# Four layers of linear and sliding-window attention with gradients, rewritten as streams of token tiles with transposes by DMA

## The chip, the cores and the metric

The kernel runs on one core of one Trainium2 chip. Times are device microseconds (us) of one execution. The kernel before takes 4126.97 us (median of 3 runs, 4115.88 to 4130.27). "PE" is the matrix engine, "PEld" its weight loads, "DVE" the vector engine, "ACT" the scalar engine, "POOL" the third elementwise engine, "SP" an engine that only issues DMAs. DMA shares are of the core's 16 DMA engines. SBUF and PSUM are the two memories in which the kernel's tiles live: DMAs load into SBUF, and PE's results go to PSUM. A "slab" is what one head group needs of q, k, v or a gradient for all tokens; the "ring" holds the transposed q, k and v of the last tiles.

## The reference

Four residual layers, A, B, A, B, on x of 2048 tokens by 640 features (32 heads of 20), with the same weights in both A layers and in both B layers. The kernel computes the output and the gradients of x and of the four weight matrices for a given output gradient, in bf16.

```python
def _A_ref(x, wqkv, wo):                    # linear attention
    q, k, v = split(x @ wqkv)               # (cut: reshape to heads)
    phi = lambda t: jnp.where(t > 0, t + 1, jnp.exp(t)) + 1e-6
    pq, pk = phi(q), phi(k)
    kv = jnp.einsum("bhsd,bhse->bhde", pk, v)
    z = jnp.einsum("bhsd->bhd", pk)
    o = jnp.einsum("bhqd,bhde->bhqe", pq, kv) / (jnp.einsum("bhqd,bhd->bhq", pq, z)[..., None] + 1e-6)
    return merge(o) @ wo

def _B_ref(x, wqkv, wo):                    # causal attention, window of 256 tokens
    scores = jnp.einsum("bhqd,bhkd->bhqk", q, k) * (Dh ** -0.5)
    mask = (idx[:, None] - idx[None, :] >= 0) & (idx[:, None] - idx[None, :] < 256)
    p = softmax(where(mask, scores, -1e9))
    return merge(jnp.einsum("bhqk,bhkd->bhqd", p, v)) @ wo

x = x + _A_ref(_layernorm(x), A_wqkv, A_wo)
x = x + _B_ref(_layernorm(x), B_wqkv, B_wo)
x = x + _A_ref(_layernorm(x), A_wqkv, A_wo)
x = x + _B_ref(_layernorm(x), B_wqkv, B_wo)
# outputs: x and, by jax.vjp with grad_out, the gradients of A_x, A_wqkv, A_wo, B_wqkv, B_wo
```

A token tile is 128 tokens, so there are 16 of them. In sliding attention a "unit" is one token tile for a group of four heads: 8 x 16 = 128 units a layer, each looking at up to three key tiles.

## The kernel before

It is a row of stages. Each stage runs over all 16 tiles and leaves its result in memory for the next one.

```python
def run(self):
    self.prep_weights()                 # pads and transposes all weights, stores them for later
    self.A_forward(0); self.B_forward(1); self.A_forward(2); self.B_forward(3)
    ...
    self.B_backward(3, first=True);  self.A_backward(2, first=True)
    self.B_backward(1, first=False); self.A_backward(0, first=False)
```

Nearly every transpose is a PE instruction into PSUM and a copy out of it. This is the one ahead of the backward projection:

```python
for f0 in range(0, QTT, fch):           # 15 blocks of 128x128 per tile, 8 per PSUM tile
    psT = pspool.tile([P, fch, P], BF, name="dqT_ps")
    self.transposes(psT, [dqkv[:, tt, f * P:(f + 1) * P] for f in range(f0, f1)])   # PE
    ...                                 # copy to SBUF by DVE or ACT
```

The exception is attention backward. There the score gradients `ds` are transposed by DMA from SP's queue, 12 blocks of 128x128 a unit, and the product that needs them comes three units after the scores:

```python
def dscore(u, half, ps):
    ...
    if half == 1:
        dsT_of[u] = pe.tile([P, 12, P], BF, name="dsT", bufs=4)
        nc.sync.dma_start_transpose(out=dsT_of[u][:, 0:4 * nkt, :], in_=ds_of[u][:, 0:4 * nkt * P])
...
load(0)                                 # seven slabs of 512 KB, from POOL's queue
for s in range(n + 3):
    if s < n and units[s][1] == 4 and units[s][0] + 1 < G:
        load(units[s][0] + 1)           # the next head group's slabs
    ...
    if 0 <= s - 3 < n:
        dq(s - 3, ps_o.tile([P, 3, 4, HPAD], F32, name="acc"))    # needs dsT of unit s-3
```

The weight gradients of each layer are computed when that layer's backward runs. The first layer of a pair writes its part to memory, the second reads it and adds.

The softmax here doesn't subtract the row's maximum and nothing guards it: scores larger than these inputs give would overflow.

## Time and profile before

The profiled execution took 4152.7 us. The table gathers the stages that the argument uses. "Busy" is the time in which an engine executed, "clock" the mean granted clock of PE as a fraction of full speed.

| stage | us | what it shows |
|---|---|---|
| whole | 4152.7 | PE 69%, DVE 51%, ACT 33%, clock 0.707 |
| sliding attention, forward, two times | 340, 360 | PE 65% and 62%, clock 0.50, DMA 0.12 and 0.15 |
| sliding attention, backward, two times | 499, 500 | PE 67%, clock 0.50, DMA 0.91 |
| one of the weight gradients | 73 | PE 91%, clock 0.94 |

The first lines of the profile's page, kernel before: busy time by engine, and the span in 40 equal slices, in tenths.

```profile
PE 2862.4 (69%) x28268; PEld 1667.8 (40%) x28268; DVE 2122.0 (51%) x5628; ACT 1367.2 (33%) x2440; POOL 428.7 (10%) x651
PEclk6978855569687555865555898689955555997799
DMA  8345611043455110489998323311599897223221
```

No engine is full over the whole. The slices with clock digit 5 are the four attention stages. Two of them coincide with a DMA row of 7 to 9 (backward), two with a row of 0 and 1 (forward). So the mean says little, and each stage is to be read by itself.

The view by window of the kernel before. Its columns are the window, its length, the busy time of PE, PEld, DVE, ACT and POOL with instruction counts, the clock, the DMA share and the bytes per time.

```profile
502.00:842.00 340.00, 220.54 (x2872) 129.63 (x2873) 187.71 (x1212) 169.10 (x128) 0.00 (x0) 0.50 0.12 37
1806.00:2305.00 499.00, 332.47 (x5344) 182.09 (x5344) 230.29 (x256) 259.38 (x641) 191.28 (x296) 0.50 0.91 158
2305.00:2378.00 73.00, 66.66 (x320) 31.67 (x321) 10.10 (x17) 0.00 (x0) 0.00 (x0) 0.94 0.16 54
```

In the backward window the only number near 1 is the DMA share. The DMA view of that same window says whose it is: the queues with their packets, megabytes and share of the 16 engines, and then the issues, with the median time to landing.

```profile
q1 hardware_dynamic: 188974, 47.92, 64.5%
q0 software_dynamic: 8064, 29.36, 25.8%
...
VT<-qkvT_131 POOLq DMA_DIRECT2D x8, 512.0 KB, 8.7
...
dsT<-ds SPq DMA_TRANSPOSE x128, 4.2
```

The first queue (SP's) carries the transposes (and one load of 2.6 MB) and the other the slab loads. Together they take 90.3% of 499 us, which is 450 us. The list of waits of PE in the window names the effect:

```profile
PE acc L875 <- DMA dsT<-ds: 114.7, 53, 9.3
PE sp L832 <- ACT e L847: 26.9, 49, 0.9
```

The columns are total us, times and the longest. PE waited 114.7 us of this stage for transposes.

### The profile page before, as it was taken

Reading aid. Unit: us, or ns where it says so; the run is one execution under the profiler, and the core shown is the slowest. Engines: PE = TensorE matmul, PEld = TensorE weight load, DVE = VectorE, ACT = ScalarE, POOL = GpSimd, SP = SyncE. Lnnn points to the kernel's source line nnn. Section 1 sums busy time; section 2 is a strip of 40 time slices with the busy share of each in tenths; the row PEclk is TensorE's granted clock in tenths of the full one; section 3 lists DMA queues with packets and bytes.
Section 4 is the critical chain, followed back from the end, with each engine's and each line's share of the span. In section 5 each row is a group of like instructions: output and inputs, shape, how many; then the busy total and the mean of one; then the engine's idle time right before and its main releaser. Section 6 shows DMA issues by size and latency. Waiting matters only on the chain. (4 is left out here: it accounts for less than half of the span.)

```text
span 4152.7 us, 70886 instructions
## 1 busy us (share of the span) xinstructions
PE 2862.4 (69%) x28268; PEld 1667.8 (40%) x28268; DVE 2122.0 (51%) x5628; ACT 1367.2 (33%) x2440; POOL 428.7 (10%) x651
## 2 busy tenths in 40 slices
PE   2767766667577666766677886578847677884577
PEld 2334433343343333433334464336423334453335
DVE  4765355556643555364445265435634444365526
ACT  1413345533033455144555120102245555120202
POOL 2000000000000000023333000000033342000000
PEclk6978855569687555865555898689955555997799
DMA  8345611043455110489998323311599897223221
GB/s 303 129 139 167 207 32 47 17 155 121 163 160 165 41 37 16 152 195 163 150 149 142 88 76 116 127 64 61 151 172 155 158 174 129 93 83 141 94 92 56
DMA packets 763051, 506.38 MB, mean 122 GB/s; under 512 B 574560, under 2 KB 728672, under 8 KB 760800
## 3 DMA queue, kind: packets, MB, share of 16 engines
q1 hardware_dynamic: 560304, 266.70, 28.4%
q10 hardware_dynamic: 186288, 176.42, 13.0%
q0 software_dynamic: 16128, 58.73, 6.1%
q8 instruction: 222, 3.64, 0.4%
q14 instruction: 109, 0.89, 0.1%
HBM read 232.72 MB, written 174.65 MB: 98 GB/s over the span
## 5 line engine op out<-in xcount | busy, mean ns | idle before, releaser
L866 DVE TENSOR_TENSOR ds<-sp,e 128x768 bf16<-128x768 f32 (+2 forms) x512 | 460.9, 907 | 516.7 <-PE sp L832 409.4
L847 ACT ACTIVATE e<-sp 128x768 bf16<-128x768 f32 (+2 forms) x512 | 392.1, 771 | 122.9 <-PE sp L832 100.6
L437 PE MATMUL sT_ps<-QTg,KTg 32*128 32x128 bf16 x2880 | 254.4, 296 | 162.0 <-DVE o_t L452 116.8
L832 PE MATMUL sp<-KT,QT 32*128 32x384 bf16 (+2 forms) x1024 | 284.7, 476 | 57.7 <-ACT e L847 32.6
L875 PE MATMUL acc<-ksl,dsT 128*128 128x20 bf16 x2880 | 124.8, 181 | 227.3 <-DMA dsT<-ds 226.9
L832 PE MATMUL sp<-VT,dOT 32*128 32x384 bf16 (+2 forms) x1024 | 246.4, 472 | 32.3 <-ACT e L847 21.1
L875 PEld LDWEIGHTS <-dsT 128*128 128x128 bf16 x2880 | 99.0, 105 | 349.5 <-DMA dsT<-ds 312.0
L551 PEld LDWEIGHTS <-dqT 128*128 128x128 bf16 x1920 | 186.3, 99 | 132.1 <-DVE dqT L545 29.9
L400 PE MATMUL qkvp_ps<-WBpad,hnT 128*128 128x512 bf16 x960 | 225.1, 386 | 1.6 <-ACT hnT L243 1.6
L851 POOL TENSOR_SCALAR_AFFINE_SELECT e<-e 128x512 bf16<-128x512 bf16 x256 | 162.1, 633 | 570.0 <-issue 525.4
L519 PEld LDWEIGHTS <-hn_bw 128*128 128x128 bf16 x1280 | 126.6, 99 | 197.4 <-issue 71.1
L547 ACT COPY dqT<-dqT_ps 128x896 bf16<-128x896 bf16 x64 | 58.0, 906 | 391.9 <-PE dqT_ps L159 304.3
L437 PEld LDWEIGHTS <-KTg 32*128 32x128 bf16 x2880 | 101.5, 112 | 198.8 <-DVE o_t L452 141.9
L291 PE MATMUL qkv_ps<-WA,hnT 128*128 128x512 bf16 (+1 forms) x640 | 149.6, 374 | 45.0 <-ACT vv L299 17.5
L551 PE MATMUL dh_ps<-WqTB,dqT 128*128 128x320 bf16 x960 | 139.6, 305 | 25.5 <-DMA WqTB<-WqTB 14.7
L551 PE MATMUL dh_ps<-WqTA,dqT 128*128 128x320 bf16 x960 | 140.4, 305 | 22.9 <-DVE dqT L545 10.3
L904 ACT ACTIVATE dqkv<-acc 128x80 bf16<-128x80 f32 x256 | 60.8, 238 | 257.9 <-PE acc L875 256.6
L855 POOL TENSOR_SCALAR_AFFINE_SELECT e<-e 128x512 bf16<-128x512 bf16 x224 | 141.8, 633 | 0.0
L875 PEld LDWEIGHTS <-e 128*128 128x128 bf16 x2880 | 103.6, 106 | 94.7 <-issue 79.5
L451 DVE RECIPROCAL linv<-sT_ps 128x4 f32<-128x4 f32 x256 | 46.8, 183 | 176.1 <-PE sT_ps L448 174.7
L875 PE MATMUL acc<-qsl,ds 128*128 128x20 bf16 x2880 | 134.0, 179 | 0.9 <-DVE ds L866 0.5
L875 PE MATMUL acc<-dosl,e 128*128 128x20 bf16 x2880 | 130.9, 181 | 4.7 <-ACT dqkv L904 4.6
(2500 smaller groups left out, 5699.9 us busy)
## 6 DMA issues: line engine op xcount, KB each, us to landing
qkvp_126<-qkvp_slab SPq DMA_DIRECT2D x16, 768.0 KB, 3.6
qkvp_130<-qkvp_slab ACTq DMA_DIRECT2D x16, 768.0 KB, 3.4
qkvT_127<-qkvT_slab ACTq DMA_DIRECT2D x32, 256.0 KB, 5.2
qkvT_131<-qkvT_slab SPq DMA_DIRECT2D x32, 256.0 KB, 4.3
dN<-tmp_dN SPq DMA_DIRECT2D x2, 2560.0 KB, 15.3
tmp_dNT<-dNT SPq DMA_DIRECT2D x2, 2560.0 KB, 7.9
dNT<-tmp_dNT ACTq DMA_DIRECT2D x2, 2560.0 KB, 13.3
WqTA<-WqTA SPq DMA_DIRECT2D x2, 2400.0 KB, 8.9
```

Source lines behind the costliest of these rows:

```text
L291: nc.tensor.matmul(ps[:, 0:w_], lhsT=hnT[:, k, tt * P:(tt + 1) * P], rhs=WA[:, k, c0:c1], start=(k == 0), stop=(k == DT - 1))
L400: nc.tensor.matmul(ps, lhsT=hnT[:, k, tt * P:(tt + 1) * P], rhs=WB[:, k, c0:c0 + 512], start=(k == 0), stop=(k == DT - 1))
L437: nc.tensor.matmul(sT[:, hh, i * P:(i + 1) * P], lhsT=KTg[HPAD * hh:HPAD * (hh + 1), kt * P:(kt + 1) * P], rhs=QTg[HPAD * hh:HPAD * (hh + ...
L519: nc.tensor.matmul(pss[m][:, 0:c1 - c0], lhsT=hn[:, tt, m * P:(m + 1) * P], rhs=dqkv[:, tt, c0:c1], start=(tt == 0), stop=(tt == TT - 1))
L551: nc.tensor.matmul(ps[:, ci, 0:cw], lhsT=dqT[:, k, :], rhs=WqT[:, k, ci * cw:(ci + 1) * cw], start=(k == 0), stop=(k == QTT - 1))
L832: nc.tensor.matmul(ps[:, j, 0:nkt * P], lhsT=slabs[g][ta][r0:r0 + HPAD, b * P:(b + 1) * P], rhs=slabs[g][tb][r0:r0 + HPAD, k0 * P:(k0 + nk ...
L847: nc.scalar.activation(ev[:, 2 * half:2 * half + 2], ps[:, :, 0:nkt * P].rearrange("p h (i k) -> p h i k", k=P), ACT.Exp, scale=c_att)
L851: nc.gpsimd.affine_select(out=ev[:, :, nkt - 1, :], in_=ev[:, :, nkt - 1, :], compare_op=ALU.is_ge, fill=0.0, base=0, pattern=[[0, 4], [-1 ...
L855: nc.gpsimd.affine_select(out=ev[:, :, 0, :], in_=ev[:, :, 0, :], compare_op=ALU.is_ge, fill=0.0, base=-1, pattern=[[0, 4], [1, P]], chann ...
L866: nc.vector.tensor_tensor(out=dv[:, hs], in0=ps[:, :, 0:nkt * P].rearrange("p h (i k) -> p h i k", k=P), in1=ev[:, hs], op=ALU.mult)
L875: nc.tensor.matmul(acc[:, slot, hh, 0:DH], lhsT=lhsT, rhs=slabs[g][rhs_name][:, t, HPAD * hh:HPAD * hh + DH], start=(i == 0), stop=(i == l ...
L904: nc.scalar.mul(dqkv[:, b, 4 * g * DH:(4 * g + 4) * DH].rearrange("p (h d) -> p h d", d=DH), acc[:, 2, :, 0:DH], c_att)
```

## The change

The intent is to let neighbouring layers share the engines. While the sliding attention of one tile runs, the projections, the norm and the next layer's qkv of other tiles fill its gaps. PE's transposes and their PSUM copies go to DMA, the weights need no preparation, and the gradients of a weight's two layers are summed in PSUM at the end. The diff is nearly a new program. Here is its core.

```diff
@@ run @@
-        self.prep_weights()
-        self.A_forward(0)
-        self.B_forward(1)
-        self.A_forward(2)
-        self.B_forward(3)
...
+            self.seg_first(acc)                       # first half of layer 0
+            for l in (0, 2):
...
+                    self.seg_pair(l, mbd, acc)        # second half of A, all of B, first half of the next A
+        self.seg_do_first(3)                          # output gradient through wo
+        for l in (3, 1):
...
+                self.seg_attention_bwd(l, dqkv)
...
+                self.seg_B_to_A(l, dqkv, acc, dNT)
+            self.seg_A_to_B(l - 1, acc, dNT)
...
+        self.weight_grads((3, 1), self.out_dWB, self.out_dWoB)
+        self.weight_grads((2, 0), self.out_dWA, self.out_dWoA)
```

The forward pair. One step handles attention of tile b, and the other work (`plan`, in this order, with its distance in tiles) is fed in two pieces per head group:

```diff
+            plan = ((qkv, 2), (first_half, -2), (proj2, -1), (proj1, 3), (mix, 4))
+            for b in range(-4, 0):
+                self.drain(step(b))
+            for b in range(TT + 2):
+                it = step(b)
+                if b < TT:
+                    o = self.B_attention(l + 1, b, slabs, ring, pw, pe, ps_s, pps,
+                                         lambda g: (next(it, None), next(it, None)))
+                self.drain(it)
```

Norm and transposes. `tr` is a DMA transpose on SP's queue. The plain stores and most loads go on ACT's:

```diff
+        hnT = pw.tile([P, self.DT, P], BF, name="ln_hnT")     # pool of two buffers
+        self.tr(hnT, hn)
+        self.dma(self.hn_d[l][:, tt, :], hn)
```

In attention backward, `dq` comes five units after the scores and there are six `dsT` buffers. `dO` is loaded once for all groups, and the other six slabs come from ACT's queue:

```diff
+        LAG = 5
-                    dsT_of[u] = pe.tile([P, 12, P], BF, name="dsT", bufs=4)
-                    nc.sync.dma_start_transpose(out=dsT_of[u][:, 0:4 * nkt, :], in_=ds_of[u][:, 0:4 * nkt * P])
+                    dsT_of[u] = pe.tile([P, 12, P], BF, name="dsT", bufs=6)
+                    self.tr(dsT_of[u][:, 0:4 * nkt, :], ds_of[u][:, 0:4 * nkt * P])
-                if 0 <= s - 3 < n:
-                    dq(s - 3, ps_o.tile([P, 3, 4, HPAD], F32, name="acc"))
+                if 0 <= s - LAG < n:
+                    dq(s - LAG)
```

The backward between attention stages, and the gradients:

```diff
+    def dh(self, l, tt, dqkv, WT, pw, pps):           # "dh": backward through qkv and the norm
+        dT = pw.tile([P, self.QTT, P], BF, name="dqkvT")
+        self.tr(dT, dqkv)
...
+    # seg_A_to_B: A_dqkv of tile tt, dh of tile tt-1, B_do of tile tt-2; weights by
+    # load_w(.., "WT"): a DMA transpose straight from the input
...
+    # weight_grads: per output, loads of both layers' operands, then for each m
+                for i in range(len(ls)):
+                    for tt in range(TT):
+                        nc.tensor.matmul(ps, lhsT=lhs[i][:, tt, m * P:(m + 1) * P], rhs=rhs[i][:, tt, :],
+                                         start=(i == 0 and tt == 0), stop=(i == len(ls) - 1 and tt == TT - 1))
```

## The prediction

> **What bounds the kernel now.** 4152.7 us profiled; no engine is full (page, part 1: PE 69%, DVE 51%, ACT 33%). It is a row of stages, each held by something else. Busy time by window:
> - 0-100 us, weight preparation and layer norm: PE 29 us busy, DMA 0.82.
> - Sliding attention forward, 502-842 and 1305-1665 (700 us): PE 65%, DVE 55%, ACT 50%, DMA 0.12, granted clock 0.50. The wait list shows PE waiting for o_t and DVE for sT_ps: a PSUM round trip limits it.
> - Other forward stages: about 1035 us.
> - Attention backward, 1806-2305 and 3010-3510 (1000 us): DMA 0.91, PE 67% at clock 0.50. In the timeline an undisturbed unit takes 2.64 us; the mean is 499/128 = 3.9. The difference is dsT: its transpose lands after 4.2 us (median, longest 18.2), slowest while the next group's slabs load, and PE consumes it one unit later. PE idles 227 us before these products.
> - Rest of the backward: about 1420 us; weight gradients are 73 us (2305-2378) plus some 22 us per layer, at clock 0.94.
>
> **What changes.**
> 1. Forward layers are fused, so attention, projections, norm and the next layer's qkv share the engines. Per tile, from durations in the trace, ACT has 8x2 exponentials of 0.81 us, about 4 us of other work and some ten DMA issues of 0.3-0.6 us: 22 us. DVE about 11 us (masks go to POOL, 0.63 us each). PE about 20 us at full clock, 35 at half. The Trainium skill ("TensorE: Matmul & The Clock Gate", Part 1) says the clock is half until sustained activity releases it; the trace agrees (0.50 in attention, 0.92-0.95 in qkv). I expect about 0.75 and 25 us a tile.
> 2. All PE transposes and their PSUM copies go to SP's DMA queue: by count about 4100 more 128x128 blocks beside 2880 for dsT. A dsT transpose of 12 blocks costs SP 1.4 us of issue; attention's SP queue share (64.5% of 499 us for 1440 blocks) is 0.22 us a block, so about 900 us of DMA time spread over the run. DMA becomes a co-limit: forward pair about 20 us a tile, A-to-B backward about 15.
> 3. Attention backward: dsT products lag five units instead of three, six dsT buffers instead of four, dO loaded once, ACT copies merged (2.2 to 2.0 us a unit). This removes the wait, not the transposes or loads: about 2.85 us a unit.
> 4. Weight gradients: same matmuls, summed in PSUM over two layers; no gain.
>
> **Estimated stages (us).** Forward 1735 -> 950 (first half-layer 120, pairs 430 and 380, closures 20). Attention backward 1000 -> 730. B-to-A 2x175, A-to-B 250+180, with norm gradients inside, and about 30 for the output gradient (largely hoisted beside the forward, as the built order shows) replace some 1040: -> 810. Weight gradients 380 -> 390. Sum **2880 us**, range **2600 to 3180**. Nearly all of it is on the critical path: the stages follow each other. Faster by over 2%: 0.96; within 2%: 0.02; slower: 0.02.
>
> **What would show it.** Forward pairs: ACT busiest, over 70%, about 25 us a tile; clock above 0.7. DMA mean share up from about 0.48 to over 0.6, SP's queue the largest. Attention backward: waits for dsT below 40 us each, unit below 3 us. Gradients: two windows near 195 us, PE over 80%.
>
> **What would make it wrong.** Transposes queueing on SP behind slab loads and stores until each tile's chain (norm, transpose, qkv, ring, attention) exceeds its lookahead; ACT blocked in order on DMA issues; PE at half clock in the fused stages (35 us a tile, +300 us); weight loads by transpose exposed at each segment start. The other way: PE at full clock in attention backward.

## The result and the profile after

The changed kernel is correct and takes 3251.23 us (median of 4 runs, 3233.28 to 3267.58), against 4128.62 us of the kernel before in its runs. The ratio is 0.7872, 95% interval 0.7821 to 0.7924, so it is faster. Here and below a ratio is the mean time of one kernel's fast runs over that of the other's of the same rounds, so it is not quite the ratio of the medians that are quoted. The time lies 71 us above the top of the predicted range and about 370 us above the predicted sum of 2880.

The page's lines for the changed kernel (profiled execution, 3231.6 us):

```profile
PE 2254.9 (70%) x24864; PEld 1335.0 (41%) x24864; DVE 1349.8 (42%) x2866; ACT 1070.0 (33%) x2105; POOL 765.8 (24%) x1280
PEclk9677877767776755555597787555557968898898
DMA  6675565367674799999997998999999799834524
```

PE works 607 us less and is no fuller: 70% after 69%. DVE lost 772 us. The DMA row is now high nearly everywhere, and a long run of 9s begins about where the backward does. The windows of the changed kernel, in order of time, columns as above:

```profile
97.00:630.00 533.00, 363.11 (x4332) 218.21 (x4333) 202.92 (x512) 245.32 (x448) 162.20 (x255) 0.76 0.57 138
630.00:1064.00 434.00, 283.32 (x3704) 160.23 (x3701) 123.37 (x316) 204.49 (x320) 157.30 (x255) 0.72 0.65 152
1064.00:1166.00 102.00, 31.68 (x160) 17.32 (x161) 47.08 (x129) 0.00 (x0) 11.22 (x19) 0.67 0.88 217
1166.00:1564.00 398.00, 326.56 (x5344) 189.97 (x5343) 230.61 (x256) 235.39 (x431) 147.44 (x240) 0.50 1.06 192
1564.00:1601.00 37.00, 0.01 (x1) 0.00 (x0) 0.00 (x0) 0.29 (x1) 5.46 (x11) 0.50 1.11 229
...
1787.00:2015.00 228.00, 149.54 (x948) 89.53 (x948) 129.44 (x368) 27.47 (x92) 28.30 (x52) 0.78 0.92 208
...
2811.00:3232.00 421.00, 355.20 (x1920) 190.26 (x1920) 21.69 (x36) 12.36 (x24) 0.00 (x0) 0.92 0.45 147
```

With the boundaries between stages read from the first and last matmul of each, the prediction can be laid beside the trace term by term. All columns are in us.

| stage | predicted | profiled | difference |
|---|---|---|---|
| first half-layer (0-97) | 120 | 97 | -23 |
| forward pair 1 (97-630) | 430 | 533 | +103 |
| forward pair 2 (630-1064) | 380 | 434 | +54 |
| closures between them | 20 | (inside the pairs) | -20 |
| output gradient (1064-1166) | 30 | 102 | +72 |
| attention backward, two times | 730 | 398 + 402 | +70 |
| B-to-A, two times | 350 | 172 + 176 | -2 |
| A-to-B, two times | 430 | 279 + 196 | +45 |
| weight gradients (2789-3232) | 390 | 443 | +53 |
| sum | 2880 | 3232 | +352 |

So the miss isn't one thing. The forward is +114, and four other terms are +45 to +72 each. What PE waits for in the first pair (changed kernel, list of waits, 97 to 630 us):

```profile
PE s L358 <- ACT e L360: 59.0, 66, 6.5
PE d L300 <- DMA ln_hnT<-ln_hn: 50.6, 16, 9.1
PE d L197 <- DMA Wo_1550<-in_A_wo_dram: 23.3, 1, 23.3
```

L300 is the qkv product of layer B. It waits 16 times, once for each tile, for the transpose of the norm's result. And in attention backward (1166 to 1564 us), the DMA view and PE's list:

```profile
q1 hardware_dynamic: 188416, 47.20, 76.2%
q10 hardware_dynamic: 38642, 28.49, 28.8%
...
dsT<-ds SPq DMA_TRANSPOSE x128, 4.9
```

```profile
PE sp L688 <- DMA VT<-qkvT_127: 39.7, 1, 39.7
PE acc L731 <- DMA dsT<-ds: 34.0, 18, 6.4
PE sp L688 <- DVE ds L721: 23.6, 51, 1.6
PE sp L688 <- ACT e L702: 7.6, 12, 3.0
```

The 39.7 us ended at 1166 and belong to the stage before. PE's waits for `dsT` fell from 114.7 to 34.0 us, as planned (e9 below shows that the lag is not all of the reason). PE also waits some 31 us for DVE and ACT. The two queues take 105% of the window by now. A sum above 100% means that records of packets overlap in part, so it is not a lower bound of the stage's time. ACT, whose queue now issues the slab loads, stands idle at its own issues:

```profile
ACT e L702 <- issue: 32.3, 14, 6.4
```

### The profile page after: what moved, and what is told of

Its sections match the earlier page's. It is cut to its first block, busy times and chain, and to the rows that moved or that the text cites. A ratio compares the mean times of both kernels' runs of the same rounds, so it can differ in the third digit from the quotient of the medians.

```text
span 3231.6 us, 61624 instructions
## 1 busy us (share of the span) xinstructions
PE 2254.9 (70%) x24864; PEld 1335.0 (41%) x24864; DVE 1349.8 (42%) x2866; ACT 1070.0 (33%) x2105; POOL 765.8 (24%) x1280
## 5 line engine op out<-in xcount | busy, mean ns | idle before, releaser
L360 ACT ACTIVATE e<-s 128x768 bf16<-128x768 f32 (+2 forms) x512 | 372.5, 771 | 200.0 <-PE s L358 109.8
L688 PE MATMUL sp<-KT,QT 32*128 32x384 bf16 (+2 forms) x1024 | 236.8, 475 | 101.3 <-DMA VT<-qkvT_127 39.7
L553 PEld LDWEIGHTS <-dqkvT 128*128 128x128 bf16 x1920 | 203.1, 107 | 249.3 <-issue 77.4
L363 POOL TENSOR_SCALAR_AFFINE_SELECT e<-e 128x512 bf16<-128x512 bf16 x256 | 163.2, 638 | 587.6 <-ACT e L360 553.3
L706 POOL TENSOR_SCALAR_AFFINE_SELECT e<-e 128x512 bf16<-128x512 bf16 x256 | 163.1, 637 | 548.9 <-issue 413.8
L688 PE MATMUL sp<-VT,dOT 32*128 32x384 bf16 (+2 forms) x1024 | 245.0, 470 | 40.1 <-DVE ds L721 21.5
L358 PE MATMUL s<-ring 32*128 32x128 bf16 x2880 | 162.7, 243 | 107.8 <-ACT e L360 98.5
L555 ACT ACTIVATE dh_junk<-d 128x320 bf16<-128x320 f32 x128 | 56.0, 437 | 496.0 <-PE d L553 479.2
L731 PEld LDWEIGHTS <-ds 128*128 128x128 bf16 x2880 | 119.0, 106 | 121.8 <-issue 116.1
L358 PEld LDWEIGHTS <-ring 32*128 32x128 bf16 x2880 | 79.8, 99 | 187.0 <-issue 171.2
L300 PEld LDWEIGHTS <-ln_hnT 128*128 128x128 bf16 x640 | 70.6, 119 | 199.8 <-DMA ln_hnT<-ln_hn 105.8
L366 POOL TENSOR_SCALAR_AFFINE_SELECT e<-e 128x512 bf16<-128x512 bf16 x224 | 144.8, 646 | 0.0
L710 POOL TENSOR_SCALAR_AFFINE_SELECT e<-e 128x512 bf16<-128x512 bf16 x224 | 142.7, 637 | 0.0
L300 PE MATMUL d<-W_1548,ln_hnT 128*128 128x480 bf16 x320 | 103.6, 499 | 50.6 <-DMA ln_hnT<-ln_hn 50.6
L501 PEld LDWEIGHTS <-gT 128*128 128x128 bf16 x640 | 65.2, 108 | 178.1 <-DMA gT<-car 138.7
```

The source lines that it names most:

```text
L300: nc.tensor.matmul(ps, lhsT=hnT[:, k, :], rhs=W[:, k, ci * 480:(ci + 1) * 480], start=(k == 0), stop=(k == self.DT - 1))
L358: nc.tensor.matmul(ps[:, j, i * P:(i + 1) * P], lhsT=ring[r0:r0 + HP, G + g, kt * P:(kt + 1) * P], rhs=ring[r0:r0 + HP, g, qs], start=True ...
L360: nc.scalar.activation(ev[:, 2 * half:2 * half + 2], ps[:, :, 0:nkt * P].rearrange("p h (i q) -> p h i q", q=P), ACT.Exp, scale=self.c_att)
L363: nc.gpsimd.affine_select(out=ev[:, :, nkt - 1, :], in_=ev[:, :, nkt - 1, :], compare_op=ALU.is_ge, fill=0.0, base=0, pattern=[[0, 4], [1, ...
L366: nc.gpsimd.affine_select(out=ev[:, :, 0, :], in_=ev[:, :, 0, :], compare_op=ALU.is_ge, fill=0.0, base=-1, pattern=[[0, 4], [-1, P]], chan ...
L553: nc.tensor.matmul(ps, lhsT=dT[:, k, :], rhs=WT[:, k, cs], start=(k == 0), stop=(k == self.QTT - 1))
```

## The experiments

All kernels are variants of the changed kernel, and differences are of medians against it (3251.23 us, ratio 0.7872) unless said otherwise. The stages' times are of the profiled run. The kernel before: 4143.31 us (e1 to e4), 4126.26 (e5 to e8), 4126.42 (e9 to e12), 4153.48 (e13 to e15), 4129.65 (e16 to e18). All results are correct except that of e4. In the profiled runs of the variants that leave the four stages between and after the attention stages alone, those stages (from the end of one attention stage to the first scores or gradient matmul of the next) add up to between 844 and 878 us, and the changed kernel has 845. So a difference of under some 30 us in one trace's sum of these stages may be spread.

### The forward pair: why 533 us and not 430?

Theory A: the chain from norm through DMA transpose to the next qkv has too little lookahead in the program order, so PE waits for it once a tile. Theory B: ACT is blocked in order behind its many DMA issues (128 between 145 and 606 us, taking 61 us), and everything behind it is late.

**e1_order** lets the next layer's first half run before the qkv product, which gives the norm's transpose more time.

```diff
-            plan = ((qkv, 2), (first_half, -2), (proj2, -1), (proj1, 3), (mix, 4))
+            plan = ((first_half, -2), (qkv, 2), (proj2, -1), (proj1, 3), (mix, 4))
```

> Only the order of the side work in a forward step changes: the next layer's qkv (tile b-2) goes first, the sliding layer's qkv (tile b+2) second, so that the norm's transpose has about 8 us to land. Only the first pair (97-606 us in the changed kernel, 27 us a steady step) is touched. Theory A (the pair is held by the chain norm, transpose, qkv at each step's start; PE waits 44 us for ln_hnT there): that wait falls below 10 us and the pair gets 40 to 90 us shorter. Rival B (the pair is held by PE work at a granted clock of 0.77): the wait goes, PE's idle time turns up elsewhere, and the pair changes by less than 15 us.

3198.04 us (3191.46 to 3220.76), ratio 0.7743: 53 us faster. In the trace of the profiled run, the last attention product of pair 1 ends 33 us earlier (577.8 after 610.7); that run as a whole is 42 us faster than the changed kernel's profiled run, so not all of the gain was placed. PE's list for that pair shows where the wait went:

```profile
PE d L212 <- DMA ln_hnT<-ln_hn: 37.1, 15, 5.9
PE d L300 <- DMA ln_hnT<-ln_hn: 24.8, 4, 9.2
```

L212 is the qkv product of the next A layer, which is now first in line. The same kind of transpose, one step too late, holds it. Reordering passes the wait from one consumer to the other and can't satisfy both.

**e2_queue** takes two kinds of stores off ACT (the `qk` rows and the transposed ring) and issues them from POOL.

```diff
-        self.dma(self.sv[l]["qk"][:, tt, :], qk)
+        self.ld(self.sv[l]["qk"][:, tt, :], qk)          # same for the three stores of the ring
```

> In both forward pairs the stores of the q/k slab and of the ring (2 per tile on average) are issued from POOL instead of ACT. ACT spends 30 us (first pair) and 21 us (second) in semaphore waits ahead of DMA issues, with idle spells of 8 us each fourth tile behind the ring store. Theory A (ACT blocked in order behind DMA issues holds the pairs): the two pairs together get 40 to 60 us shorter. Rival B (ACT has slack, 51% busy): within 15 us; or slower, as POOL's masks now wait behind those stores.

3252.92 us, ratio 0.7864: no change. ACT's time in issuing between 145 and 606 us fell from 61 to 38 us, and its time at semaphores ahead of issues from 28 to 1 us, while PE waited for `ln_hnT` 60.7 us where it had waited 50.6. The 40 to 60 us that B expected are not there: ACT did wait for its issues, but little hung on it. The test is not quite clean, because stores from POOL's queue may have slowed the transposes by the 10 us (compare e9).

**e7_lead** gives both transposes one more step: `proj1` and `mix` a tile earlier, `first_half` a tile later, and four buffers for `ln_hnT`.

```diff
-            plan = ((qkv, 2), (first_half, -2), (proj2, -1), (proj1, 3), (mix, 4))
-            for b in range(-4, 0):
+            plan = ((qkv, 2), (first_half, -3), (proj2, -1), (proj1, 4), (mix, 5))
+            for b in range(-5, 0):
-            for b in range(TT + 2):
+            for b in range(TT + 3):
-        hnT = pw.tile([P, self.DT, P], BF, name="ln_hnT")
+        hnT = pw.tile([P, self.DT, P], BF, name="ln_hnT", bufs=4)
```

> Forward pairs: both norms are made one step earlier (out-projection of tile b+4, mix of b+5, next layer's qkv of tile b-3, four buffers for the transposed norm), so no matmul needs a transpose of the step before. Theory A (exposed norm and transpose): waits of PE for ln_hnT, 44 us before and 43 us with the mere reordering, fall below 8 us in each pair; first pair 40 to 70 us shorter than 533, second 20 to 50 shorter than 432, less a fill longer by one step. Rival B (PE throughput at the granted clock, and the imbalance of ACT work within a step): the waits go, but the pairs change by under 15 us each.

3146.92 us (3138.98 to 3155.94), ratio 0.7628, interval 0.7601 to 0.7654: 104 us faster. The window of pair 1, and PE's list for it:

```profile
97.00:525.00 428.00, 336.06 (x4336) 201.15 (x4336) 203.74 (x524) 241.44 (x448) 161.99 (x256) 0.85 0.74 173
```

```profile
PE s L358 <- ACT e L360: 27.2, 15, 5.9
PE d L197 <- DMA Wo<-in_A_wo_dram: 23.3, 1, 23.3
PE d L197 <- DMA oT<-o_t: 16.6, 6, 6.0
```

Pair 1 takes 428 us (it was 533, and 430 had been predicted), with the same work. The waits for `ln_hnT` are gone from the top of the list, and the clock rose from 0.76 to 0.85, so that PE's busy time for nearly the same instructions (4336 after 4332) fell from 363 to 336 us. Theory A holds for pair 1. Pair 2 stayed at 432 us. PE waits there 64.2 us, 16 times, for `oT`, the transpose ahead of the last projection:

```profile
PE d L197 <- DMA oT<-o_t: 64.2, 16, 6.5
```

**e11_lead2** does the same for that one: `proj2` two tiles after attention in the last pair, and four `oT` buffers.

```diff
-            plan = ((qkv, 2), (first_half, -3), (proj2, -1), (proj1, 4), (mix, 5))
+            plan = ((qkv, 2), (first_half, -3), (proj2, -2 if last else -1), (proj1, 4), (mix, 5))
+        # oT: bufs=4 in the last pair
```

> As the one-step lead, and in the second pair the second out-projection also follows attention by two tiles, with four buffers for its transposed input. With the lead alone the second pair stayed at 432 us and PE waited 47 us there for oT. Theory A (exposed transposes): this wait falls below 10 us and the second pair to 375 to 405 us. Rival B (PE and ACT taking turns at half clock within a step): 420 us or more.

3102.88 us (3098.85 to 3110.13), ratio 0.7524, interval 0.7506 to 0.7542: another 44 us. Pair 2 takes 403 us, and the forward ends at 935 us. The prediction had said 950, with errors that offset each other (97 for 120 in the first half-layer, 403 for 380 in pair 2). So the forward's sizes were about right for a program whose lookahead and buffers cover a DMA transpose, and the changed kernel's don't.

### Attention backward: why 400 us and not 365?

The rival theories: A, PE at half clock with its waits; B, the DMA time of the transposes together with the loads. Counting the packets' time in the trace of the changed kernel, divided by 16 engines: transposes 184320 packets of 256 B at 26.1 ns, 300 us; slab loads and stores on ACT's queue 49 + 15 + 50, about 115 us. Together 415 us, against a stage of 398. The mean unit is 398/128 = 3.1 us.

**e4_noload** loads the slabs of the first head group only. Its results are wrong (relative error 6.8), and its instructions are otherwise the same. With the loads go 42 of the 52 DMA issues that ACT makes in the stage.

```diff
             def load(g):
+                if g:
+                    slabs[g] = slabs[0]
+                    return
                 r = {}
```

> Wrong results on purpose: attention backward loads the slabs of the first head group only and reuses them for all eight, so 42 of 48 slab loads per stage go and the dsT transposes stay. Rival B of the run before (DMA holds the stage): each stage falls from 400 us to 330 to 360. Theory A (PE at half clock): it falls by under 25 us, because PE waits for dsT only 34 us per stage.

3152.16 us, ratio 0.7622: 99 us faster, the two attention stages 349.6 and 348.5 us (48 and 53 us less). This is the size that B expected. PE's list and ACT's idle time at issues in the first stage, and the view by window inside it:

```profile
PE acc L734 <- DMA dsT<-ds: 13.3, 7, 7.0
PE sp L691 <- DVE ds L724: 9.3, 24, 0.8
PE sp L691 <- ACT e L705: 4.3, 11, 2.4
ACT e L705 <- issue: 1.5, 5, 0.4
```

```profile
1200.00:1500.00 300.00, 280.02 (x4749) 166.31 (x4745) 203.64 (x227) 210.35 (x384) 130.13 (x214) 0.50 0.93 152
```

Of the 48 us, PE's waits for `dsT` give 21 (34.0 to 13.3), its waits for DVE and ACT some 18 (31.2 to 13.6), and its shorter busy time 11 (327 to 316); the list leaves out waits under 0.15 us, so the parts fit only roughly. The loads bring two things that this run removes together: DMA time beside the transposes, and ACT's idle time at its issues (32.3 to 1.5 us). It shows what the loads cost, not that DMA time alone is the reason. PE is busy 93% here, still at clock 0.50, and a unit takes 2.73 us. Without the loads PE takes over as the limit. So 2.85 us a unit, the predicted size, is reached only without the loads that the prediction had left in.

**e3_dense2** adds two matmuls of 352 columns per unit whose result nobody reads. A longer busy PE might be granted its full clock, or PE's extra time might show that PE limits.

```diff
                 dsT = dsT_of.pop(u)
+                for _ in range(2):
+                    nc.tensor.matmul(dqa[:, 160:512], lhsT=dsT[:, 0, :], rhs=dO[:, 0, 0:352], start=True, stop=True,
+                                     skip_group_check=True)
```

> Attention backward gets two extra matmuls of 352 columns per unit into unused PSUM columns (results unread). Theory A (PE work at half clock holds the stage: PE 82% busy at 0.50): if the clock stays at 0.50 the extra 0.6 us of PE per unit lengthens each of the two stages from 400 us by 50 to 75 us; if the clock rises instead, they shorten. Rival B (the DMA engines hold it, share 1.06): less than 20 us change.

3298.15 us, ratio 0.7975. The stages grow from 398 to 424 and from 402 to 426 us. The extra PE time in the window is 381.87 - 326.56 = 55 us, so half of it is hidden. This lies between the two theories. It fits PE and the loads holding the stage together, each showing only in part while the other is left: PE's waits for `dsT` were 18 us here, after 34.

```profile
1170.00:1590.00 420.00, 381.87 (x5580) 206.31 (x5579) 230.85 (x256) 236.46 (x431) 146.88 (x240) 0.50 1.01 180
```

PE is busy 91% for 420 us and the clock stays at 0.50.

**e8_spread** loads the next group's six slabs one a unit instead of all at once. If the burst of loads were the trouble, this would help.

```diff
-                if s < n and units[s][1] == 6 and units[s][0] + 1 < G:
-                    load(units[s][0] + 1)
+                if s < n and units[s][1] == 6 and units[s][0] + 1 < G:
+                    loads = load(units[s][0] + 1)        # now a generator, one slab a step
+                if s < n and units[s][1] >= 6 and units[s][0] + 1 < G:
+                    next(loads, None)
```

> Attention backward: the six slab loads of the next head group are issued one per unit (units 6 to 11) rather than in one burst at unit 6; same bytes. Without the loads a stage took 350 us, with them 400. Theory A (the burst delays the dsT transposes past their slack of five units): most of the 50 us come back, stage 355 to 375. Rival B (the DMA engines have no room for the loads at any time): stage within 10 us of 400.

3262.85 us, ratio 0.7908; stages 405 and 407 us. No gain, so the burst is not the trouble.

**e9_poolload** issues the loads from POOL's queue, as the kernel before did, to take their issue time off ACT.

```diff
-                    self.dma(r[n], sv["qkvT"][:, i * G + g, :], nc.scalar)
+                    self.dma(r[n], sv["qkvT"][:, i * G + g, :], nc.gpsimd)      # and the other slabs
```

> Attention backward issues its slab loads from POOL's queue, as the kernel before did, instead of ACT's; same bytes, same burst. Without the loads a stage took 350 us, with them 400, spread or not. Theory A (ACT's own time: each issue costs ACT 0.35 to 0.7 us in order, 48 per stage, and PE, at 93% busy without loads, starves behind late exponentials): stage 360 to 375. Rival B (the loads slow the dsT transposes in the DMA engines): stage within 10 us of 400, waits for dsT as before (35 us).

3316.77 us, ratio 0.8041: 66 us slower, stages 427 and 422 us. The same loads from POOL's queue cost the transposes more. PE's waits in the first attention stage of e9:

```profile
PE acc L731 <- DMA dsT<-ds: 77.4, 28, 10.6
PE sp L688 <- ACT e L702: 13.5, 22, 0.8
PE sp L688 <- DVE ds L721: 4.9, 16, 0.8
```

The waits for `dsT` were 34.0 us in the changed kernel. Those for ACT and DVE fell from 31.2 to 18.4 us, which may come of the issues taken off ACT, or only of PE being held longer by the transposes. So this run can't rule out that ACT's issues are a part of what the loads cost. The longest landing of a `dsT` transpose in that stage was 20.6 us, against 10.0 us with ACT's queue, and 18.2 us in the kernel before, which loaded from POOL too. Of the 81 us by which the change shortened PE's waits for `dsT` in this stage, 43 therefore go with the queue of the loads and not with the five-unit lag. The Trainium skill ("DMA: Bandwidth & Descriptors", Issuing engines are not separate DMA queues) says that all DMAs run on the same 16 engines, whichever engine started them, and that issuing from several engines only saves issue time. By that alone the queue should not matter to the transposes; in this case's traces it does: 398 against 427 us for the same loads. Why POOL's queue disturbs the transposes more was not settled.

**e13_layout** stores `qk` by head group, so that those loads are runs of 4 KB a partition instead of 256 B pieces: far fewer packets, the same bytes.

```diff
-                qk=d.tile([P, TT, 2 * H * HP], BF, name=f"qk{l}"),
+                qk=d.tile([P, 2 * self.G, TT, P], BF, name=f"qk{l}"),
-                    self.dma(r[n], sv["qk"][:, :, (i * G + g) * P:(i * G + g + 1) * P], nc.scalar)
+                    self.dma(r[n], sv["qk"][:, i * G + g, :, :], nc.scalar)
```

> The q and k of the sliding layers are stored head group by head group, so that attention backward's q and k slabs load in runs of 4 KB a partition instead of sixteen runs of 256 bytes; same bytes, and the forward stores now have the short runs. Theory A (packet count: the two slabs are 4096 of the load's short packets per group): each attention stage 400 to 365 to 385 us, forward pairs within 15 us. Rival B (bytes and the competition as such): each stage within 8 us of 400.

3282.02 us, ratio 0.7911; stages 402 and 408 us. No gain in the stage, so the count of the loads' packets is not what the transposes suffer from: PE's waits for `dsT` were 50 us, after 34. The kernel as a whole is 31 us slower by the medians, but the intervals of the ratios overlap. In the trace its second forward pair ends 25 us later, which is more than the 15 us allowed for; the first, which stores the same short runs, ends 2 us later, so the reason is open.

### The stages between: the dqkv transposes, the weights' transposes, the lag

**e5_petr** gives the transposes of `dqkv` back to PE, with PSUM copies on DVE and ACT. If DMA held the stages between attention, they would get shorter. If PE did, they would get longer by some 30 us.

```diff
-        self.tr(dT, dqkv)
+        for f0 in (0, 8):
+            f1 = min(self.QTT, f0 + 8)
+            pT = pps.tile([P, 8, P], BF, name="tps", bufs=2)
+            for f in range(f0, f1):
+                nc.tensor.transpose(pT[:, f - f0, :], dqkv[:, f * P:(f + 1) * P], self.ident)
+            ...                                            # copy to dT by DVE or ACT
```

> Undoes one part of the change: in the backward norm step the 15 blocks of dqkv per tile are transposed by PE again, with a copy out of PSUM on DVE and one on ACT (two PSUM banks set aside for it), not by DMA. Theory A (the backward segments are held by DMA: share 0.92 to 1.06 in the A-to-B segments, dqkv's transpose lands after 7.1 us there): the two A-to-B segments (279 and 196 us) together get 30 to 70 us shorter, the B-to-A segments stay within 15 us. Rival B (the DMA transposes are hidden; PE and DVE hold these segments): the four segments together get 30 us longer or more, since each tile gains about 1.2 us of PE and 0.7 us of DVE.

3247.83 us, ratio 0.7866, interval 0.7841 to 0.789: nothing. The DMA share of the first A-to-B fell from 0.92 (1.00 in its first 51 us) to 0.72 without a gain, and the four stages together are about 13 us longer, which is within their spread. For these transposes DMA and PE are a wash. The window of that stage in e5:

```profile
1735.00:2015.00 280.00, 182.35 (x1332) 114.87 (x1329) 160.88 (x443) 45.04 (x117) 42.32 (x70) 0.82 0.72 171
```

**e6_prep** transposes the weights once, in pieces at the heads of the steps of the second forward pair, stores them, and loads them plainly later. The trace had shown idle starts of B-to-A: in the window 1564 to 1601 above PE executes one instruction in 37 us, and the transpose of `wqkv` straight from the input landed there only after 31.7 us.

```diff
-            self.tr(t, self.Wqkv[kind])
+            self.dma(t, self.wT_d[kind, "WT"])
...
+                for _ in range(3):                         # at the head of each step of the last pair
+                    c = next(chunks, None)
+                    if c is not None:
+                        wt = pw.tile([P, 1, self.D], BF, name="wt_prep")
+                        self.tr(wt, c[1])
+                        self.dma(c[0], wt[:, 0, :])
```

> Restores weight preparation: the transposed weights are made once, five blocks at a time beside the last forward pair, stored, and loaded plainly at the start of each backward segment. Theory A (the idle stretches before the backward segments, 37, 51, 40 and 49 us with PE almost unused, are the weights' DMA transpose from HBM, 19 to 31 us to land, holding the one transpose queue): the four stretches fall by 50 to 80 us together and the second forward pair grows by less than 15 us. Rival B (they are pool turnover and the closing chain of the linear layer): less than 20 us.

3251.16 us, ratio 0.788: no change in sum. The four idle starts shrank by some 50 us together (the first from 37.4 to 21.6, so moving the transpose took away less than half of it), the four stages as a whole by 20, and pair 2 grew by 36 us. The transposes were moved from an idle stretch into one where they were in the way.

**e10_ablag** lets A-to-B run `dh` two tiles behind instead of one and `B_do` four instead of two.

```diff
-                t = tt - 1
+                t = tt - 2
                 if 0 <= t < self.TT:
                     self.dh(l, t, dq.pop(t), WT, pw, pps)
...
-                t = tt - 2
+                t = tt - 4
```

> A-to-B segments: the norm gradient follows dqkv by two tiles instead of one, the next layer's output gradient by four instead of two, with one more dqkv buffer. Taking the dqkv transposes off DMA left these segments (279 and 196 us) as long as they were. Theory A (each tile waits for transposes of the tile before: lookahead too short, as in the first forward pair): the two together get 40 to 90 us shorter. Rival B (throughput of DVE and DMA): less than 15 us, or longer by the two more fill steps.

3209.38 us, ratio 0.778: 42 us faster. In the trace, the two A-to-B stages, the second up to the gradients' first matmul, shrink from 279 and 218 to 265 and 195 us, which is 37, and PE's waits there for `gT` and `dqkvT` fall from 103 to 52 us. It is the forward's cause again: a DMA transpose (`gT`, `dqkvT`) consumed too soon.

### The weight gradients, and versions that join the gains

**e12_all** joins e11, e9 and e10 with five buffers in the output-gradient stage, `dO` loaded after the slabs, and opposite sides of SBUF for the two phases of the gradients.

```diff
-            pw = self.pool(st, "bpw", 2)                  # output-gradient stage
+            pw = self.pool(st, "bpw", 5)
-            self.dma(dO, sv["dO"])                        # attention backward: ahead of load(0)
             load(0)
+            self.dma(dO, sv["dO"])
-                    pW = self.pool(s2, "wg")              # gradients; pw too
+                    pW = self.pool(s2, "wg", side="left" if srcs is self.hn_d else "right")
```

> The edits of the three runs before together, and three more whose stages are apart: five instead of two buffers for the output gradient ahead of the first attention backward (102 us from the end of the forward to attention's first scores), the slab loads ahead of the load of dO, and the two phases of each weight gradient on opposite sides of SBUF. If the stages add up: forward about 910 us, gap before attention 70 to 85, attention 2 x 370, A-to-B shorter by 40 to 90, weight gradients 400 to 425 instead of 442; in all 2930 to 3020 us, below both kernels. If they compete for DMA instead: above 3080.

3121.18 us, ratio 0.7545, interval 0.7508 to 0.7583: no better than e11 alone (0.7524), with four more edits in it. The attention stages took 432 and 438 us, again with POOL's loads.

**e14_best** is e12 with the slab loads back on ACT's queue.

> Forward leads, A-to-B lags, deeper buffers ahead of the first attention backward, dO loaded after the first slabs, weight gradients on two sides of SBUF; slab loads on ACT's queue as in the change. If the stages add: e11's 3103 us less about 33 (A-to-B), 5 to 15 (gap), 10 (gradients): 3040 to 3065 us. If they compete: 3090 or more.

3077.57 us (3069.37 to 3079.44), ratio 0.7412. The output-gradient stage with its wait for loads fell from 102 to about 85 us. Of the four exposed loads of the gradients, opposite sides hid only one by half. The time lies between the two forecasts (3040 to 3065 if the gains add, 3090 or more if they compete), so they add in part.

**e15_best2** is e14 with the diff of e13 and with that of e6, its loop moved from the heads of the steps to their ends and with two pieces a step (three in every fourth).

> The former with the q and k layout and the weights' transposes made two or three chunks at the end of each step of the second pair. If the idle stretches before the backward segments shrink by 46 us as in e6 and the second pair grows by less than 15, and the layout gives 15 to 35 us per attention stage: 2950 to 3010 us. If the transposes again hold the pair's own (36 us) and the layout gives nothing: 3030 to 3060.

3077.52 us, ratio 0.7421: the same as e14. The idle starts are shorter, and the second pair ends at 980 us instead of 930; 14 us of that are already there at the end of the first pair's attention.

What holds the gradients' loads? PE's list for the gradients of the changed kernel (2811 to 3232 us):

```profile
PE wg L873 <- DMA wg_r_36558<-dqkv_113: 22.4, 1, 22.4
PE wg L873 <- DMA wg_r_37690<-dqkv_112: 21.8, 1, 21.8
PE wg L873 <- issue: 20.2, 1, 20.2
PE wg L873 <- DMA wg_r_37306<-g_109: 20.0, 1, 20.0
```

That is one wait at the head of each of four phases, 84 us. Two things could hold the loads: the memory that they land in, which the phase before occupies, or ACT's program order, in which the loads stand behind that phase's last copies and stores.

**e16_gsp** moves the loads to SP's queue, which is idle there. **e17_gsides** moves them and gives the two phases of each call opposite sides of SBUF. **e18_best3** is e14 with the loads from SP.

```diff
-                        self.dma(t, srcs[l])
+                        self.dma(t, srcs[l], nc.sync)                            # e16, e17, e18
-                            self.dma(t, right[l][:, :, c0:c0 + width])
+                            self.dma(t, right[l][:, :, c0:c0 + width], nc.sync)
-                    pW = self.pool(s2, "wg")
+                    pW = self.pool(s2, "wg", side="left" if srcs is self.hn_d else "right")   # e17, e18; pw too
```

> The changed kernel with the gradients' loads issued from SP instead of ACT, nothing else. If memory alone holds the loads (each phase reuses the memory of the one before), the four waits of 20 to 22 us stay and the time is within 10 us of the changed kernel. If ACT's program order alone holds them, three of the four waits vanish and it is 45 to 65 us faster. If both hold them, nothing is gained here and only the next run gains.

3245.43 us, ratio 0.7836: the four waits stay at 22.2, 21.5, 22.4 and 21.2 us.

> As the run before, and the two phases of each call on opposite sides of SBUF. If both memory and ACT's program order hold the loads: three of the four waits vanish or fall below 8 us each, the gradients' stage falls from 442 us (with its idle start) to about 385, and the kernel is 45 to 65 us faster than the changed kernel. If something else holds them (the loads' own time against a phase's length), the gain is below 15 us, as with opposite sides alone.

3235.84 us, ratio 0.7826. From the first gradient matmul to the last it is 400 us instead of 417: a gain of 17 us, far below the 45 to 65 of the case where both hold the loads and nothing else. PE's list for the gradients of e17:

```profile
PE wg L873 <- issue: 44.9, 3, 17.9
PE wg L873 <- DMA wg_r<-dqkv: 22.1, 1, 22.1
```

The three later waits are 17.4, 17.9 and 9.6 us, and the trace ties them to the landing of the preceding phase's stores. The queue alone gives nothing (e16), the sides alone gave about 10 us of shorter waits (within e14), both give 17. So both play a part, and neither is most of it: 67 of the 84 us of waits remain, and what holds them was not found. One candidate is the memory still: by the tiles' sizes in the code, the two phases and the constants come to about 220 KB a partition, and the two sides may overlap. This last step was argued from sizes and not tried.

> The best version so far (3077.6 us) with the gradients' loads from SP. If the loads were held by ACT's program order: about 3025 us, with 3010 to 3045 holding it. If not: 3077 again.

3036.98 us (3031.67 to 3042.99), ratio 0.7347, interval 0.7319 to 0.7374. It beats both kernels. Its time lies in the range forecast for ACT's program order, but by luck: the stretch of the gradients' matmuls shrank by 9 us only (400 after 409). The rest of its gain over e14 (ratio 0.7412) is in the four stages between attention, some 37 us shorter in its trace (807 after 844; e12, with the same code there, has 820). Between the two attention stages PE, DVE, ACT and POOL execute the same instructions in the same order in both traces, and that stretch is 20 us shorter all the same; after the second attention stage DVE's order differs. So the cause stays open, and the two versions ran on different chips.

## Why the prediction was wrong, point by point

The direction and the kind of gain were right. The total fell outside the range, because five terms of the sum were too small. The largest of them, the forward pairs, is the step that failed: a DMA transpose was priced by what it occupies, and not by the time that its consumer waits for it.

- **Forward pairs, "430 and 380", "25 us a tile".** They were 533 and 434. The failed step is the assumption that a step lasts about as long as its busiest engine works (ACT, 22 us a tile, "busiest, over 70%"), with nothing added for waits. ACT was busy 46% of pair 1 and PE 68%; what was left was waiting. The prediction had named the reason among its risks ("until each tile's chain (norm, transpose, qkv, ring, attention) exceeds its lookahead") and not priced it. e7 and e11 bring the pairs to 428 and 403 us by lookahead and the buffers for it alone, so it is shown. The rival risk, "ACT blocked in order on DMA issues", gave none of its 40 to 60 us in e2. The clock (predicted 0.75, measured 0.76 and 0.72) was right, though partly by luck: once the waits were gone it was 0.85 in pair 1 (e7).
- **Output gradient, "about 30, largely hoisted".** It was 102 us. The step that failed is the reading of the built order: what stood early there were DMA issues into a tile that lives throughout, while PE's work of this stage starts only after the last work of the pair. That it waits for the pair's memory is argued from the program's pools and was not tested. In the stage, 27 us of PE's wait go to transposes of the gradient with two buffers, and 40 us to the first loads of attention.
- **Attention backward, "about 2.85 us a unit", 730.** It was 3.1 us and 800. "This removes the wait, not the transposes or loads" was written down and then not costed: the DMA view of the kernel before held 64.5% + 25.8% of 499 us = 450 us of DMA time in the stage. The estimate of 365 us has no term for it. After the change the packets add up to 415 us in 398. The predicted waits for `dsT` (below 40 us) were right at 34, but partly by luck: with the lag and POOL's queue they were 77 (e9), and the prediction doesn't mention the move of the loads to ACT's queue. e4 shows that without the loads the stage is 350 us, that is, that they cost about 50; how much of it is DMA time and how much ACT's issuing was not separated. e8, e9 and e13 show that spreading them, moving their issue to POOL or making their packets larger doesn't give it.
- **A-to-B, "250+180".** It was 279 and 196. e10 gets some 37 us back by lag, with the same instructions and one buffer more. The weights' transposes exposed at a segment's start, a named risk too, are in the trace as idle starts (37 and 40 us before B-to-A), of which e6 could take 16 and 19, but only by paying in the pair.
- **Weight gradients, "380 -> 390", "same matmuls".** They were 443 us. The matmul stretches themselves fell from 372 us (sum of eight in the kernel before) to 355 (sum of four). The missing term is four exposed loads, 84 us. What holds them is open (e16, e17). The kernel before had `dqkv` in SBUF when it needed it; the change gave that up.
- **DMA, "over 0.6", "0.22 us a block".** The queues' shares come to 78%. The transposes take 898048 packets, which are 7016 blocks (predicted about 6980), and 1415 us of 16 engines' time: 0.20 us a block. This term was right, including that DMA becomes a co-limit. In e5 a lower DMA share in A-to-B gained nothing, so a high share alone does not mark the limit.
- **B-to-A, "2x175".** 172 and 176 us. Right in sum, but 37 and 40 us of it are idle starts, which the estimate didn't contain; the work itself is faster than expected, so the match is partly luck.

One rule for reading follows. The prediction costed each stage as the larger of its engines' times and left the exposure at the seams as risks. In a program of eleven segments the seams (idle starts, first loads, a transpose consumed a step too early) were most of the 350 us by the table; the loads in attention backward (70 us) are not one of them.

## What to carry to other kernels

When a transpose goes from PE to DMA, it can change from a cost into a latency, as it did here: move its consumer one step further away and give it a buffer more, or PE pays for it once a tile (here 105 us in one pair, got back with more lookahead and buffers, without removing an instruction). Add up the DMA time that a stage keeps, transposes and loads together, before predicting it from its compute engines. Work moved into a "free" stretch, such as the weights' transposes into the forward pair, is free only if the engine that takes it is not on the chain there.

## What the Trainium skill lacked or had wrong

- "TensorE: Matmul & The Clock Gate", Part 1, says that the clock is released after about 3.4 us of sustained activity. In attention backward the trace does not show it. In e3 PE was busy 91% of 420 us, with stretches of up to 30.7 us without a gap over 20 ns between matmuls (by the trace's ends, which are modelled), and the granted clock stayed at 0.50. In e4 it was 93% busy at 0.50. In the weight gradients it was 0.92. The prediction's "the trace agrees" holds for the shares that it quotes, and not for the rule. What tells them apart the page doesn't say; the matmuls of this stage are narrow (32 rows of weights, or 20 columns of output), but wide dummies in e3 did not release it either.
- "DMA: Bandwidth & Descriptors", Issuing engines are not separate DMA queues: the same slab loads beside a stream of transposes cost 398 us of stage from ACT's queue and 427 from POOL's, with 34 and 77 us of waits for the transposes. That section speaks of issue time only. Elsewhere the same page calls DMAs from SP and ACT generally faster, so the direction is no contradiction; it has no figure for loads beside transposes.
- The same page, Latency and other measured facts, gives a DMA transpose an effective 261 GB/s with a non-contiguous middle dimension, and more without. Here the 128x128 blocks between SBUF tiles moved 47.2 MB in 300 us of all 16 engines' time, about 157 GB/s; and a transpose of 640x1920 bf16 straight from an input, 2.46 MB, landed after 31.7 us, under 80 GB/s, beside other traffic.
- The same page has no figure for what ordinary loads cost a stream of DMA transposes: without the loads (94 us less of DMA time, and 32 us less of ACT's issuing) PE's waits for the transposes fell from 34.0 to 13.3 us and the stage by 48 (e4), while changing the loads' packet size (e13) or spacing (e8) gave nothing.
